# Top-k attention with a GELU layer on one Trainium2 core: last query rows squared on DVE and turned over through DRAM

## The chip, the core and the metric

The kernel runs on one core of a Trainium2 chip. The core has five engines that run side by side, each through its own list of instructions in order: TensorE (PE, matmuls and transposes; its weight loads are shown as PEld), VectorE (DVE), ScalarE (ACT), GpSimd (POOL) and SyncE (SP). Here SP does little but issue DMA transfers, one after another; an issue that has to wait for another engine holds back every later issue in SP's list. The metric is the device time of one execution in microseconds (us), lower being better. Times of the kernel before: 1479.85, 1480.17 and 1480.43 us.

## What is computed

Two blocks in a row, all in float32. The first is attention that keeps, for each query row, only the 32 largest of its 576 scores; the second is a two-layer network with an exact GELU.

```python
B, H, S, D = 8, 8, 576, 64
scores = (1 / sqrt(D)) * q @ k.T                     # per batch and head, 576 x 576
kth    = 32nd largest of each row
scores = where(scores >= kth, scores, -1e9)
attn   = exp(scores - row max) / (row sum + 1e-9)
x      = (attn @ v), heads side by side              # (8 * 576) x 512
out    = gelu(x @ w_in) @ w_out                      # 512 -> 2048 -> 512
```

## The kernel before

**Items.** A batch has 8 heads, taken as 4 pairs. The 576 query rows of a head are cut into four blocks of 128 (`t` = 0 to 3, `NM` = 4) and a last block of 64 (`TL`). An item of the list `items` is one tile of scores with 128 partitions and 2 x 576 columns (`s`, 1152 columns): for `t < NM` one block of 128 rows of the two heads of a pair, side by side. The 64 last rows of a head fill only half the partitions, so a last item (`t == NM`) takes two pairs, `r` = 0 and 1, each with two heads, `e` = 0 and 1: four quarters of 64 partitions by 576 columns. Head `e` of pair `r` stands in the partitions `half(r, e)`, the lower half where `r == e`. In the kernel before, the columns are divided by pairs: columns 0 to 575 hold pair 0, columns 576 to 1151 pair 1.

There are 144 items, 18 for a batch. Two batches make a ring of 36 items; the first batch of a ring has its two last items at the end, the second at its beginning, so four last items stand one behind the other: items 16 to 19 of each ring of 36, which over the kernel are 16 to 19, 52 to 55, 88 to 91 and 124 to 127.

**Slots.** The program is written out by hand in slots: the loop `for n in range(ahead)` emits, for each engine, the work of slot `n`. In slot `n`, DVE finds the 32 largest scores of item `n` (`top_k`: rounds of MAX8 and MATCH_REPLACE8, with the row's smaller and larger halves sorted apart first by `larger` on DVE and `sum_up` and `smaller` on POOL). ACT makes item `n-1` into exponentials (`select`, `softmax`) and POOL completes its row sums (`add_small`). At the end of `top_k(n)` DVE takes the reciprocal of those sums (`inverse(n-1)`, L504), which waits for POOL's L510 and through it for ACT; behind it POOL scales item `n-1` (`normalise`, L552). So DVE and POOL start each slot together, at the reciprocal. PE makes the scores of items `n+2` and `n+3` in even slots (`scores`, L386 and L401, copied from PSUM to `s` by ACT in L394 and L406), and turns over item `n-2` (`transposes`), since the product with v needs the probabilities with keys on partitions. What is left of PE's time goes to the pieces of the network (`mlp`: `h_ps` in L773, `seven` and `y_ps` in L927 and L929), a given number for each slot.

**Turning over.** There are two ways. By PE: eight 128 x 128 transposes (L649), a transpose of the tail columns (L619, or two of 64 columns in L622 for a last item), and copies by ACT to the tile `pt` (L664, L629; the tails of a last item go in two copies, L635, to a tile of their own, `pt_end`). Or, where `squared(i)` holds, by DVE and DRAM: `square_p` transposes 32 x 32 squares within `s` on DVE (L569, in the middle of `top_k` of slot `i+2`), `write_p` sends the tile to DRAM in four DMAs (L579, at the end of slot `i+2`), and `read_p` brings it back with its squares in order in four more (L586, at the beginning of slot `i+3`). Before the change `squared(i)` holds for every other item with `t < NM` from item 28 on, 48 in all. `pt` has one buffer; it holds two items with `t < NM` (one squared, one turned over by PE), whose product `attend` (L715) follows in the slot after.

**The product of a last item.** `attend(n-3)` in slot `n` multiplies `pt` and `pt_end` with v, two heads of two pairs (L726), and ACT copies the result to `xT` (L731, `copy_x`). For the first batch of a ring it then loads v of the same pairs of the next batch into the same tiles (`issue(load("v", ...))`), eight DMAs on SP (L131, L134) for an item. `issue` runs a load at once, unless `held[0]` is set: in a slot whose item `n-2` is squared, loads wait in `late_issues` until `flush()`, behind `write_p(n-2)`.

**PSUM.** The transposes, the products, `seven` and the tail scores share one bank in turn (`bank`, tag "z"); the first scores of a slot use tag "pr", the second scores (`second=True`) and `h_ps` share tag "l1".

Of the kernel before, what the change touches and what calls it, by code (L numbers as in the profile page):

```python
# [14 lines left out]
def kernel(  # L15
# [19 lines left out]
    nc = tc.nc  # L35
    f32, i32, u32 = mybir.dt.float32, mybir.dt.int32, mybir.dt.uint32
    bf16, i16, u16 = mybir.dt.bfloat16, mybir.dt.int16, mybir.dt.uint16
    AF = mybir.ActivationFunctionType
# [295 lines left out]

        return slice((r ^ e) * TL, ((r ^ e) + 1) * TL)

    def halves(t, e, step):

        return spread(t[:, e * TL :], step + (TL if e == 0 else -TL), TL)

    def pair_tile(name, tag="pr"):
        return ps.tile([P, 2, 512], f32, tag=tag, bufs=1, name=name)

    def last_keys(i, t_ps):

        pair, t = items[i]
        s = S_of[i]
        if t < NM:
            nc.tensor.matmul(
                t_ps[:, 0:P], lhsT=q_of[pair][:, t * P : (t + 1) * P],  # L350
                rhs=kt_of[pair][:, SM : SM + P], start=True, stop=True,
            )
            if i == 0:
                return lambda: nc.vector.tensor_scalar(
                    s[:, SM : S + TL], t_ps[:, 0:P], scale, None, op0=ALU.mult
                )
            return lambda: nc.scalar.activation(
                s[:, SM : S + TL], t_ps[:, 0:P], func=AF.Copy, scale=scale
            )
        for r in range(2):  # L360
            kt = kt_of[pair + r]
            for e in range(2):
                nc.tensor.matmul(
                    t_ps[half(r, e), r * TL : (r + 1) * TL],
                    lhsT=kt[:, SM + P + e * TL : SM + P + (e + 1) * TL],
                    rhs=kt[:, SM + e * TL : SM + (e + 1) * TL],
                    start=True, stop=True,
                )
        return lambda: nc.scalar.activation(
            s.rearrange("p (r n) -> p r n", r=2)[:, :, SM:S],  # L370
            t_ps[:, 0:P].rearrange("p (r n) -> p r n", r=2), func=AF.Copy, scale=scale,
        )

    def scores(i, second=False):
        if i >= N or i in S_of:
            return
        pair, t = items[i]
        S_of[i] = s = work.tile([P, 2 * S], f32, tag="s", bufs=6, name="s")
        s_ps = pair_tile("s_ps", "l1" if second else "pr")
        if not few[0]:  # L380
            last_keys(i, bank("t_ps"))()
        if t < NM:
            q_t, kt = q_of[pair][:, t * P : (t + 1) * P], kt_of[pair]
            for e in range(2):
                rows = slice(e * D, (e + 1) * D)
                nc.tensor.matmul(  # L386
                    s_ps[:, e], lhsT=q_t[rows, :], rhs=kt[rows, 0:SM], start=True, stop=True
                )
# [5 lines left out]
            nc.scalar.activation(spread(s, S + TL, SM), s_ps, func=AF.Copy, scale=scale)  # L394
# [12 lines left out]

    lists_of = {}
    HS = S // 2
# [171 lines left out]
    def read_p(i):  # L581

        if squared(i):
            d = turned.pop(i)
            for k in range(P // SQ):
                nc.sync.dma_start(  # L586
                    out=pt_now[0][k * SQ : (k + 1) * SQ, :, 0:P], in_=d[:, :, k, :]
                )

    def transposes(i):  # L590
# [14 lines left out]
        def tails(ahead):  # L605
# [1 line left out]
            keys = last_keys(ahead, tp) if ahead is not None and ahead < N else None  # L607
            at = P
            if t % 2 == 0:
                pt_now[0] = work.tile([P, 2 * NM + 1, 2 * P], f32, tag="pt", bufs=1, name="pt")  # L610
            if diag is not None:
                for e in range(2):
                    nc.tensor.matmul(
                        tp[e * TL : (e + 1) * TL, at : at + P],
                        lhsT=s[:, SM + e * TL : SM + (e + 1) * TL], rhs=diag[:, e],
                        start=True, stop=True,
                    )
            elif t < NM:
                nc.tensor.transpose(tp[:, at : at + P], s[:, SM : S + TL], ident)  # L619
            else:  # L620
                for r in range(2):
                    nc.tensor.transpose(  # L622
                        tp[0:TL, at + r * P : at + (r + 1) * P],
                        s[:, r * S + SM : (r + 1) * S], ident,
                    )
            if keys:
                keys()
            if t < NM:
                nc.scalar.copy(  # L629
                    out=pt_now[0][:, NM, t % 2 * P : (t % 2 + 1) * P], in_=tp[:, at : at + P]  # L630
                )
                return
            for e in range(2):
                c = slice(e * TL, (e + 1) * TL)
                nc.scalar.copy(  # L635
                    out=halves(pt_end[c, 0, :], e, P),
                    in_=halves(tp[0:TL, at : at + 2 * P], e, P),
                )

        x = t % 2 * P if t < NM else 0  # L640

        def turn_over(tp, e):
            first = e * (S + TL if t < NM else S)
# [52 lines left out]
    def attend(i):  # L696
# [24 lines left out]
        else:  # L721
            for r in range(2):
                vt = raw_of("v", pair + r)
                for j in range(NJ):
                    for e in range(2):
                        nc.tensor.matmul(  # L726
                            o[e * D : (e + 1) * D, r * TL : (r + 1) * TL], lhsT=vt[:, j, e, :],
                            rhs=pt[:, r * NJ + j, half(r, e)] if j < NM else pt_end[:, r, half(r, e)],
                            start=(j == 0), stop=(j == NJ - 1),
                        )  # L730
            copies.append(lambda: nc.scalar.copy(  # L731
# [588 lines left out]
```

## Time and profile before

| | |
|---|---|
| median of 3 runs | 1480.17 us |
| profiled execution, its own time | 1479.73 us |
| its span | 1478.0 us |
| busy time of PE, DVE, ACT, POOL | 1461.6, 1294.3, 1099.9, 1140.1 us |
| DMA packets, bytes | 477645, 112.94 MB |
| share of 16 DMA engines that SP's queue took | 35.3% |

The span runs from the first to the last instruction; the 1.7 us between it and the time of that execution lie around it. In the profile, "L649" is a line of the kernel before; a row names the engine, the operation, the tile written and the tiles read, and the shape. Rows of the timeline begin with the start in us from the start of the span and the time that the instructions took together; a bracket at the end tells how long the engine had been idle and which engine's instruction ended that. A float32 matmul shows as two records (x2), a transpose as one. A row of windows gives the length of a stretch and then the busy time of each engine in it.

### The profile page before, as it was taken

What the parts mean: (1) busy time and instruction counts of PE and PEld (TensorE: products, weight loads), DVE (VectorE), ACT (ScalarE), POOL (GpSimd) and SP (SyncE); (2) the same over time, 40 slices, a digit from 0 to 9 for tenths busy, and PEclk for the clock granted to TensorE, in tenths of its full rate; (3) what the DMA queues carried; (4) which work ended last, traced back from release to release, by engine and by line L of the source; (5) the groups of instructions that cost most, each with busy time, mean ns of one, the idle gap of its engine ahead of it and who ended that gap; (6) DMA issues with size and microseconds to landing.
All of it is one profiled execution on the core that took longest, in us unless ns stands there. A gap on an engine that the chain in (4) does not pass through costs nothing. (4 is left out here: it accounts for less than half of the span.)

```text
span 1478.0 us, 27006 instructions
## 1 busy us (share of the span) xinstructions
PE 1461.6 (99%) x8817; PEld 1147.9 (78%) x8817; DVE 1294.3 (88%) x3318; ACT 1099.9 (74%) x1942; POOL 1140.1 (77%) x1291
## 2 busy tenths in 40 slices
PE   8999999999999999999999999999999999999999
PEld 6876677877777777887777778787777777787787
DVE  8999899999999988999999987999999997998701
ACT  7999977877777687777777778777777777776620
POOL 6877567877898879877898978886788887987732
PEclk9999999999999999999999999999999999999999
DMA  7424310045435322345534331345453421233300
GB/s 198 143 86 124 84 48 1 24 88 101 95 73 93 66 58 52 65 95 108 105 83 81 69 61 47 66 93 99 97 103 73 89 55 41 61 61 72 70 15 15
DMA packets 477645, 112.94 MB, mean 76 GB/s; under 512 B 413216, under 2 KB 469056, under 8 KB 477504
## 3 DMA queue, kind: packets, MB, share of 16 engines
q1 hardware_dynamic: 476240, 110.78, 35.3%
q8 instruction: 70, 1.15, 0.3%
q14 instruction: 71, 0.58, 0.1%
q10 hardware_dynamic: 1200, 0.39, 0.1%
q0 software_dynamic: 64, 0.03, 0.0%
HBM read 73.39 MB, written 37.75 MB: 75 GB/s over the span
## 5 line engine op out<-in xcount | busy, mean ns | idle before, releaser
L773 PE MATMUL h_ps<-xT,w_in_sb 128*128 128x256 f32 (+1 forms) x2560 | 536.2, 361 | 0.1
L773 PEld LDWEIGHTS h_ps<-xT,w_in_sb 128*128 128x128 f32 x2560 | 436.5, 190 | 73.4 <-issue 25.2
L483 DVE MAX8 top<-lists 128x8 f32<-128x576 f32 (+1 forms) x792 | 476.4, 641 | 0.0
L486 DVE MATCH_REPLACE8 lists<-top,lists 128x288 f32<-128x288 f32 (+1 forms) x528 | 307.9, 589 | 0.0
L552 POOL TENSOR_TENSOR s<-s,rden 128x1152 f32<-128x1152 f32 x135 | 285.8, 2117 | 0.3 <-DVE rden L504 0.3
L529 ACT ACTIVATE s<-s,bias 128x576 f32<-128x576 f32 x288 | 225.4, 787 | 11.0 <-issue 0.4
L517 ACT ACTIVATE s<-s,neg 128x576 f32<-128x576 f32 x288 | 225.5, 793 | 1.7 <-POOL neg L497 1.6
L510 POOL TENSOR_SCALAR den<-den 128x2 f32<-128x2 f32 x144 | 31.4, 218 | 215.9 <-ACT s L529 210.2
L455 POOL TENSOR_TENSOR lists<-lists 128x576 int32<-128x576 int32 x132 | 186.2, 1410 | 4.0
L447 POOL TENSOR_TENSOR lists<-s 128x576 int32<-128x576 int32 x133 | 187.2, 1407 | 0.0
L715 PE MATMUL o<-pt,raw_v 128*64 128x256 f32 x1280 | 153.0, 384 | 1.8 <-ACT s L529 1.1
L715 PEld LDWEIGHTS o<-pt,raw_v 128*64 128x64 f32 x1280 | 87.8, 136 | 85.8 <-issue 37.2
L789 ACT ACTIVATE g<-h_ps 128x512 f32<-128x512 f32 x144 | 78.2, 594 | 100.6 <-PE h_ps L773 100.4
L929 PE MATMUL y_ps<-w_out_sb,sum 128*128 128x256 f32 x472 | 140.4, 379 | 0.0
L394 ACT ACTIVATE s<-s_ps 128x1024 f32<-128x1024 f32 x127 | 125.5, 1035 | 10.5 <-PE s_ps L386 10.3
L664 ACT COPY pt<-tp 128x1024 f32<-128x1024 f32 x85 | 86.6, 1019 | 62.2 <-PE tp L649 62.1
L386 PE MATMUL s_ps<-kt,qm 64*128 64x512 f32 x512 | 129.4, 618 | 0.8 <-ACT s L392 0.8
L504 DVE RECIPROCAL rden<-den 128x2 f32<-128x2 f32 x144 | 23.2, 161 | 108.6 <-POOL den L510 107.4
L486 DVE MATCH_REPLACE8 lists<-first,lists 128x288 f32<-128x288 f32 x264 | 114.3, 439 | 0.0
L929 PE MATMUL y_ps<-w_out_sb,g 128*128 128x256 f32 x480 | 113.4, 379 | 0.0
L483 DVE MAX8 first<-lists 128x8 f32<-128x288 f32 x268 | 106.6, 436 | 0.0
L929 PEld LDWEIGHTS y_ps<-w_out_sb,g 128*128 128x128 f32 x480 | 91.2, 190 | 12.4
(167 smaller groups left out, 2533.1 us busy)
## 6 DMA issues: line engine op xcount, KB each, us to landing
turned<-s SPq DMA_DIRECT2D x192, 144.0 KB, 3.5
pt<-turned SPq DMA_DIRECT2D x192, 144.0 KB, 3.2
raw_v<-in_v_dram SPq DMA_DIRECT2D x64, 128.0 KB, 2.4
out_dram<-y SPq DMA_DIRECT2D x30, 256.0 KB, 2.1
raw_q<-in_q_dram SPq DMA_DIRECT2D x112, 64.0 KB, 2.0
raw_k<-in_k_dram SPq DMA_DIRECT2D x112, 64.0 KB, 2.0
w_out_sb<-in_moe_w_in_dram SPq DMA_DIRECT2D x14, 511.8 KB, 4.8
w_out_sb<-in_moe_w_out_dram SPq DMA_DIRECT2D x10, 511.8 KB, 4.1
```

Source lines behind the costliest of these rows:

```text
L386: nc.tensor.matmul(s_ps[:, e], lhsT=q_t[rows, :], rhs=kt[rows, 0:SM], start=True, stop=True)
L394: nc.scalar.activation(spread(s, S + TL, SM), s_ps, func=AF.Copy, scale=scale)
L447: nc.gpsimd.tensor_tensor(t[:, :, 1].bitcast(i32), a.bitcast(i32), b.bitcast(i32), op=ALU.add)
L455: nc.gpsimd.tensor_tensor(into_of(i)[:, :, 1].bitcast(i32), both, top, op=ALU.subtract)
L483: nc.vector.max(x[:, e], src[:, e])
L486: nc.vector.match_replace(dst[:, e], x[:, e], src[:, e], LOWEST)
L517: nc.scalar.activation(s, s, func=AF.Prelu, bias=st["neg"][:, e : e + 1], scale=1.0, alpha=STEEP)
L529: nc.scalar.activation(s, s, func=AF.Exp, bias=st["bias"][:, e : e + 1], scale=1.0, accum_out=st["den"][:, e : e + 1],)
L552: nc.gpsimd.tensor_tensor(s, s, wide, op=ALU.mult)
L715: nc.tensor.matmul(o[e * D : (e + 1) * D, 0:n], lhsT=vt[:, j, e, :], rhs=pt[:, e * NJ + j if j < NM else NM, :], start=(j == 0), stop=(j = ...
L773: nc.tensor.matmul(h_tile(u)[:, i, :], lhsT=w_in_sb[:, ko, f * P : (f + 1) * P], rhs=xT[:, ko, c0 : c0 + n], start=(ko == 0), stop=(ko == ...
L929: nc.tensor.matmul(acc[names][:, k], lhsT=lhsT, rhs=rhs, start=(j == 0 and k == 0), stop=(j == FT // 2 - 1 and k == 1),)
```

## The change

`squared(i)` now also holds for the last items between item 27 and item 141, that is for twelve of the sixteen (items 52 to 55, 88 to 91 and 124 to 127), besides the 48 from before. For these items `delayed(i)` holds too: `attend(n-4)`, ahead of `read_p` and of the scores in slot `n`, takes the place of `attend(n-3)`, behind the scores. `read_p` now takes the tile `pt` itself, where before the slot of `transposes` did.

For the squares to come out in the order that `read_p` expects, the columns of a last item now hold heads instead of pairs: columns 0 to 511 are head 0, 512 to 639 the tails of both heads, 640 to 1151 head 1, as in the other items. `scores`, `last_keys`, `attend` and `transposes` follow that. The tail of a last item is then one block of 128 columns, turned over by one PE transpose and one copy into `pt` where PE does it (items 16 to 19), and `pt_end` with its memset goes.

```diff
     def last_keys(i, t_ps):
...
-                    t_ps[half(r, e), r * TL : (r + 1) * TL],
+                    t_ps[half(r, e), e * TL : (e + 1) * TL],
...
-            s.rearrange("p (r n) -> p r n", r=2)[:, :, SM:S],
-            t_ps[:, 0:P].rearrange("p (r n) -> p r n", r=2), func=AF.Copy, scale=scale,
+            s[:, SM : S + TL], t_ps[:, 0:P], func=AF.Copy, scale=scale
...
     def scores(i, second=False):
...
-                        s_ps[half(r, e), r, :], lhsT=kt[rows, SM + P + e * TL : SM + P + (e + 1) * TL],
+                        s_ps[half(r, e), e, :], lhsT=kt[rows, SM + P + e * TL : SM + P + (e + 1) * TL],
...
-            s2 = s.rearrange("p (r n) -> p r n", r=2)
-            nc.scalar.activation(s2[:, :, 0:SM], s_ps, func=AF.Copy, scale=scale)
+            nc.scalar.activation(spread(s, S + TL, SM), s_ps, func=AF.Copy, scale=scale)
...
-    pt_end = const.tile([P, 2, P], f32, name="pt_end")
-    nc.gpsimd.memset(pt_end, 0.0)
 
     def squared(i):
 
-        return SINGLE.stop - 2 < i < N - 2 and i % 2 == 0 and items[i][1] < NM and i % RINGS != 12
+        if not SINGLE.stop - 2 < i < N - 2:
+            return False
+        return items[i][1] == NM or (i % 2 == 0 and i % RINGS != 12)
+
+    def delayed(i):
+
+        return squared(i) and items[i][1] == NM
+
+    def pt_tile():
+        return work.tile([P, 2 * NM + 1, 2 * P], f32, tag="pt", bufs=1, name="pt")
...
         if squared(i):
             d = turned.pop(i)
+            pt_now[0] = pt_tile()
...
             def keys_only(ahead):
-                pt_now[0] = work.tile([P, 2 * NM + 1, 2 * P], f32, tag="pt", bufs=1, name="pt")
...
-            elif t < NM:
+            else:
                 nc.tensor.transpose(tp[:, at : at + P], s[:, SM : S + TL], ident)
-            else:
-                for r in range(2):
-                    nc.tensor.transpose(
-                        tp[0:TL, at + r * P : at + (r + 1) * P],
-                        s[:, r * S + SM : (r + 1) * S], ident,
-                    )
...
-            for e in range(2):
-                c = slice(e * TL, (e + 1) * TL)
-                nc.scalar.copy(
-                    out=halves(pt_end[c, 0, :], e, P),
-                    in_=halves(tp[0:TL, at : at + 2 * P], e, P),
-                )
+            nc.scalar.copy(out=pt_now[0][:, NM, x : x + P], in_=tp[:, at : at + P])
...
-                            rhs=pt[:, r * NJ + j, half(r, e)] if j < NM else pt_end[:, r, half(r, e)],
+                            rhs=pt[:, e * NJ + j if j < NM else NM, half(r, e)],
...
         held[0] = n < N and squared(n - 2)
+        product = delayed(n - 4) and attend(n - 4)
         read_p(n - 3)
...
-        product = attend(n - 3)
+        if not delayed(n - 3):
+            product = attend(n - 3) or product
```

In the lists of instructions that the two programs give to the engines, this is what comes of it for items 52 to 55 (the other two groups alike). PE loses ten transposes an item; the pieces of the network stay in the slots in which they were; the product of each item stands a slot later, and in the even slots it stands ahead of the two items' scores, with L773 directly behind them. SP's list, which held sixteen v loads and two stores of `y` here, becomes (W for the four DMAs of `write_p`, R for the four of `read_p`, V for eight loads of v, by item): W52, R52, W53, R53, W54, V, R54, W55, V, two stores of `y`, R55, W56. POOL's list stays as it was but for the memset.

More of the change, by code (lines that the diff above doesn't have):

```diff
@@ L335, in half @@
         return slice((r ^ e) * TL, ((r ^ e) + 1) * TL)
-    def halves(t, e, step):
-        return spread(t[:, e * TL :], step + (TL if e == 0 else -TL), TL)
     def pair_tile(name, tag="pr"):
@@ L609, in tails @@
             if t % 2 == 0:
-                pt_now[0] = work.tile([P, 2 * NM + 1, 2 * P], f32, tag="pt", bufs=1, name="pt")
+                pt_now[0] = pt_tile()
             if diag is not None:
@@ L617, in tails @@
                     )
-            elif t < NM:
+            else:
                 nc.tensor.transpose(tp[:, at : at + P], s[:, SM : S + TL], ident)
-            else:
-                for r in range(2):
-                    nc.tensor.transpose(
-                        tp[0:TL, at + r * P : at + (r + 1) * P],
-                        s[:, r * S + SM : (r + 1) * S], ident,
-                    )
             if keys:
                 keys()
-            if t < NM:
-                nc.scalar.copy(
-                    out=pt_now[0][:, NM, t % 2 * P : (t % 2 + 1) * P], in_=tp[:, at : at + P]
-                )
-                return
-            for e in range(2):
-                c = slice(e * TL, (e + 1) * TL)
-                nc.scalar.copy(
-                    out=halves(pt_end[c, 0, :], e, P),
-                    in_=halves(tp[0:TL, at : at + 2 * P], e, P),
-                )
-        x = t % 2 * P if t < NM else 0
+            nc.scalar.copy(out=pt_now[0][:, NM, x : x + P], in_=tp[:, at : at + P])
+        x = t % 2 * P
         def turn_over(tp, e):
-            first = e * (S + TL if t < NM else S)
+            first = e * (S + TL)
             for j in range(NM):
```

## The prediction, made before the changed kernel ran

> **What bounds the kernel now.** I read the page first, for the busy times; then windows of busy time over the five slots around items 52 to 55; then the timeline of each engine there.
>
> ```profile
> PE 1461.6 (99%) x8817; PEld 1147.9 (78%) x8817; DVE 1294.3 (88%) x3318; ACT 1099.9 (74%) x1942; POOL 1140.1 (77%) x1291
> ```
>
> PE is busy 99% of the span. A busy PE is not always a full one, so the slots decide.
>
> ```profile
> core 0: us, PE busy (x) PEld busy (x) DVE busy (x) ACT busy (x) POOL busy (x), PEclk, DMA share, GB/s
> 526.87:536.93 10.06, 10.06 (x64) 8.27 (x58) 8.09 (x23) 6.46 (x13) 9.35 (x12) 1.00 0.05 8
> 536.93:549.24 12.31, 12.31 (x107) 9.61 (x107) 8.09 (x23) 10.44 (x23) 5.91 (x7) 1.00 0.22 50
> 549.24:559.51 10.27, 10.25 (x116) 8.97 (x113) 8.10 (x23) 7.05 (x15) 10.03 (x13) 1.00 0.27 60
> 559.51:569.65 10.14, 10.14 (x58) 7.78 (x58) 8.09 (x23) 9.53 (x18) 9.98 (x13) 1.00 0.14 53
> 569.65:578.89 9.24, 9.24 (x79) 8.24 (x76) 9.24 (x24) 6.59 (x13) 8.53 (x10) 1.00 0.29 44
> ```
>
> These are slots 54 to 58, cut at DVE's reciprocals. In slots 54 to 57 items 52 to 55 go over PE: PE never waits, DVE works only 8.09 us of each. Slot 58 has a square and DVE fills it: 9.24 us. POOL fills slots 56 and 57 (10.03 of 10.27, 9.98 of 10.14), which no saving elsewhere can shorten. The rows that show the join of the engines:
>
> ```profile
> 536.76 0.17 DVE L504 RECIPROCAL rden<-den 128x2 f32<-128x2 f32 x1 [1.97 <-POOL den L510]
> 549.07 0.17 DVE L504 RECIPROCAL rden<-den 128x2 f32<-128x2 f32 x1 [4.22 <-POOL den L510]
> 573.39 1.36 DVE L569 STREAM_TRANSPOSE s<-s 128x1152 f32<-128x1152 f32 x1
> 536.51 0.22 POOL L510 TENSOR_SCALAR den<-den 128x2 f32<-128x2 f32 x1 [0.55 <-ACT s L529]
> ```
>
> DVE waits 1.97 us in slot 54 and 4.22 in slot 55 for sums that come late over ACT from PE; in slot 54 POOL itself waits only 0.55. So there is room for a square on DVE in these slots, and PE is the bound.
>
> **What PE is spared.** An item's transposes, from start to the next start:
>
> ```profile
> 543.14 0.38 PE L622 MATMUL tp_t<-ident,s 128*64 128x128 f32 x2
> 543.36 0.60 PE L929 MATMUL y_ps<-w_sum,sum 128*128 128x256 f32 x2
> ...
> 544.22 1.04 PE L649 MATMUL tp<-ident,s 128*128 128x128 f32 x8
> 545.10 0.60 PE L929 MATMUL y_ps<-w_sum,g 128*128 128x256 f32 x2
> ```
>
> 0.22 + 0.88 = 1.10 us an item, 4.4 us for each group of four, 13.2 us in all. Items 16 to 19 lose one transpose of 0.11 us each, 0.4 us; DVE waits little there, so I take 0.3 (between 0 and 0.4). POOL's memset goes at the start, under loads: nothing. ACT's copies go with the transposes; they only shorten ACT.
>
> **What DVE pays.** Slot 58 against 8.09 us of work: 9.24 - 8.09 = 1.15 us a square. Slot 54 then ends when POOL lets it, 0.5 us sooner (at 536.4); slot 55 takes 9.25 instead of 12.31 and ends at 545.65, 3.6 us sooner; slots 56 and 57 stay at POOL's 10.27 and 10.14, which hide the squares, and end at 555.9 and 566.1.
>
> **Where the product comes.** It is no longer made from what ACT copied, but from what eight DMAs bring. PE's rows for the product, the scores and what follows, and ACT's copies of the scores:
>
> ```profile
> 546.92 1.99 PE L386 MATMUL s_ps<-kt,qm 64*128 64x512 f32 x8
> ...
> 557.80 0.69 PE L726 MATMUL o<-pt,raw_v 128*64 128x64 f32 x16
> ...
> 559.12 1.13 PE L773 MATMUL h_ps<-xT,w_in_sb 128*128 128x256 f32 x4
> 560.08 1.03 PE L927 MATMUL seven<-w_sum,g 128*128 128x256 f32 x4
> ...
> 567.54 1.99 PE L386 MATMUL s_ps<-kt,qm 64*128 64x512 f32 x8
> 569.45 0.69 PE L726 MATMUL o<-pt,raw_v 128*64 128x64 f32 x16
> ...
> 570.77 2.86 PE L773 MATMUL h_ps<-xT,w_in_sb 128*128 128x256 f32 x12
> ...
> 573.68 4.48 PE L773 MATMUL h_ps<-xT,w_in_sb 128*128 128x256 f32 x20
> 578.00 1.03 PE L927 MATMUL seven<-w_sum,g 128*128 128x256 f32 x4
> ```
>
> ```profile
> 568.71 1.94 ACT L394 ACTIVATE s<-s_ps 128x1024 f32<-128x1024 f32 x2 [0.21 <-PE s_ps L386]
> ```
>
> A product takes 1.32 us (569.45 to 570.77; likewise 557.80 to 559.12). Today it also covers something: the second scores share the PSUM tag "l1" with `h_ps`, so L773 must wait for the second L394, which ends at 570.65, while the product runs until 570.77. With the product ahead of the scores that cover is gone: 3.23 us from the first scores to L773 (567.54 to 570.77), of which the scores themselves are 1.91 (to 569.45). So PE newly waits 1.3 us in slots 56 and 58.
>
> SP's rows for the transfers (the first two from a place where four v loads, for one pair, stand behind a write; then the eight of an item, here and in the next ring):
>
> ```profile
> 325.04 0.90 SPq L131 DMA_DIRECT2D raw_v<-in_v_dram  x1
> ...
> 327.58 0.51 SPq L134 DMA_DIRECT2D raw_v<-in_v_dram  x1
> ...
> 537.89 0.39 SPq L131 DMA_DIRECT2D raw_v<-in_v_dram  x1
> ...
> 542.97 0.47 SPq L134 DMA_DIRECT2D raw_v<-in_v_dram  x1
> ...
> 567.12 1.05 SPq L844 DMA_DIRECT2D out_dram<-y  x2
> 574.82 3.40 SPq L579 DMA_DIRECT2D turned<-s  x4
> 580.89 2.55 SPq L586 DMA_DIRECT2D pt<-turned  x4
> ...
> 885.97 0.39 SPq L131 DMA_DIRECT2D raw_v<-in_v_dram  x1
> ...
> 890.13 0.47 SPq L134 DMA_DIRECT2D raw_v<-in_v_dram  x1
> ```
>
> ```profile
> 1390.89 2.54 SPq L586 DMA_DIRECT2D pt<-turned  x4
> ```
>
> ```profile
> 1396.21 2.16 PE L715 MATMUL o<-pt,raw_v 128*64 128x256 f32 x18 [1.08 <-ACT s L529]
> ```
>
> A write starts 574.82 - 569.65 = 5.17 us after its slot; a read can start 580.89 - 574.82 = 6.07 after the write, when that has landed; a product can start 5.32 us after the read's first issue (1390.89 to 1396.21: PE waits there, and ACT, which the bracket names, had nothing to do with `pt` of a squared item). SP needs 3.40 us to issue a write, 2.55 for a read, 1.05 for the stores. Eight v loads take 5.55 (537.89 to 543.44) or 4.63 (885.97 to 890.60), and four behind a write 3.05 (325.04 to 328.09), so that eight behind a write (V) lie between 4.6 and twice 3.05, 6.1. I take 5.35, the middle. With gaps of 0.05 between groups:
>
> - Item 52: write at 526.87 + 5.17 = 532.0, read at 538.1, product from 543.4. PE, with 2.2 us saved and one product less ahead, is there at 546.92 - 2.2 - 1.32 = 543.4. No wait.
> - Item 53: write at 536.4 + 5.17 = 541.6, read 547.65, product from 553.0. PE: from 543.4 on the 10.88 us that now lie between 546.92 and 557.80, less 1.1, plus 1.3 to 2.0 for ACT's copies (the second waits until write 53 has landed and freed its `s`): 555.1. No wait.
> - Item 54: write at 545.65 + 5.17 = 550.8, issued until 554.25. Now V stands ahead of the read, since the load is held until behind the write: 554.3 to 559.65. Read at 559.7, though the data had landed at 556.9; product from 565.0. PE: 555.1 + 9.74 - 1.1 = 563.75. **Wait 1.25 us.**
> - Item 55: SP is free at 562.3, write until 565.75, V until 571.15, stores until 572.25, read 572.3, product from 577.6. PE: 565.0 + 1.32 + 3.23 + 2.91 + 0.8 of 4.32 = 575.95. **Wait 1.65 us.**
>
> The product ends at 578.95, the last L773 takes 0.96 (559.12 to 560.08), and L927 starts at 579.9, where it starts at 578.00 now: 1.9 us later. Of that, a wait that PE has today a little further on goes away:
>
> ```profile
> 581.46 0.38 PE L349 MATMUL tp_t<-kt,qm 128*128 128x128 f32 x2
> 581.97 0.33 PE L619 MATMUL tp_t<-ident,s 128*128 128x128 f32 x1
> ```
>
> 581.97 - 581.46 - 0.22 = 0.3 us. **Net 1.6 us later for each group of four.** From there PE sets the pace as before, and DVE, 3.4 us ahead, waits for it. The chain that decides is SP's: from write 54 to product 55 it is issue after issue with no gap, while the 4.4 us saved on PE become waits for `pt` and for ACT's copies.
>
> The sum: 3 x 1.6 - 0.3 = +4.5 us against the profiled execution's own 1479.73 us, so 1484.2; the median of the runs lies 0.44 above that execution, so **1484.6 us** (+0.3%). The bounds of V (4.6 to 6.1, two of them a group) move it by -4.5 and +4.5: 1480 to 1489.
>
> **A rule weighed.** The first matmuls of the kernel stand in the trace at another rate than the later ones of the same shape:
>
> ```profile
> L1113 PE MATMUL warm<-ident x276: 275/275/377, 15.2 to 92.3; 128*128 128x128 f32 x138
> L1113 PE MATMUL warm<-raw_v x18: 421/421/580, 1.0 to 4.8; 128*128 128x128 f32 x18
> ```
>
> They are slow until some 5 us, and no later wait here (1.08 us at 1396.21) brought the slow rate back. The Trainium skill, page "TensorE: Matmul & The Clock Gate", section "Part 1: The HAM clock gate (the "warmup" mystery)", says that an idle window of about 3.4 us puts PE back to half rate. By it the waits of 1.3 to 2.0 us forecast here would not trip the gate and the sum stays 1484.6; two waits running into one would, which is rival (d) below.
>
> **Rivals.** (a) *The reads are in time.* If SP gets through V in 3.9 us or less each (5.35 less half of the 1.25 + 1.65), or PE comes later than I think, only the waits for ACT's copies remain: 4.4 - 2 x 1.3 = 1.8 us gained a group, and the 0.3 at L619: 3 x 2.1 + 0.3 = 6.6 us, 1473.6. For it: items 52 and 53 are in time in my own sum. Against it: V stands in SP's list between W54 and R54, and 3.9 us is below the shortest of today's rows. (b) *The gain is had in full*, to what DVE and POOL allow: 3.4 us a group, 1480.2 - 10.5 = 1469.7. It needs (a) and L773 not held by ACT's copies; the tag speaks against it. (c) *It cancels*: a chain 1.5 us shorter than mine, 1480. (d) *Slower, by PE's clock*: if a wait reaches the point where PE slows (the waits for 54 and ACT's copies in slot 58 joining past 3 us), each group has matmuls at 421 instead of 275 ns for some 4 us, as at the start, 1.4 us or more for each of two waits: 3 x 2.8 more, 1493. The granted clock is 1.00 in all rows today, and the forecast waits are half as long. (e) *Late reads run on into slot 60*: write 56 can only start behind read 55, at 574.9, its product at 586.3, where PE comes some 3 us later; it takes 3 us more of delay than forecast to begin, so little chance, and 3 x 3 us more: 1493.6. That the change doesn't do what it says (twelve squares) has next to no chance: SP's list shows the DMAs.
>
> **How the numbers follow.** Forecast 0.61, (a) 0.14, (b) 0.04, (c) 0.10, (d) 0.06, (e) 0.05. The forecast's own range is 1480 to 1489; most of (a) lies below, so the range goes from 1476 to 1490. About 0.2%, 3 us, is what can be told from no change. Faster by more: (a) nearly all and (b), 0.17. Within 3 us of 1480.2: (c), and the lower third of the forecast's range, whose upper limit is 1483.1: 0.27. Slower: the rest, 0.56.
>
> **What would show it.** Sixty squares of 1.36 us; DVE's waits at the reciprocal in slots 54 to 57 gone but for POOL's. PE waits of 1 to 2 us ahead of L726's products of items 54 and 55 of each group, none ahead of 52 and 53; L773 idle 1.3 us behind the scores of slots 56 and 58, released by ACT. On SP, reads 54 and 55 issued the moment the v loads and stores end, though their writes landed earlier; then a wait of DVE of some 5 us in slot 59. If the reads start at their writes' landing instead, or PE's idle time in slots 54 to 59 adds up to less than 4.4 us a group, the forecast is wrong and (a) is right. If PEclk drops, (d).

## The result, and the profile after

The changed kernel takes 1490.20 us (median of 4 runs, 1489.46 to 1490.83) against 1480.30 us (1479.85 to 1480.84) for the kernel before, run beside it: a ratio of 1.0067, with a 95% interval of 1.0049 to 1.0084. It is slower by about 9.9 us, where 4.4 were forecast. Its profiled execution took 1489.96 us, 10.2 more than the one before, and that is the difference taken apart here.

Windows over the slots 54 to 59 of the kernel after, cut at DVE's reciprocals as before (length, then busy time of PE, PE's weight loads, DVE, ACT and POOL, then the clock granted to TensorE):

```profile
core 0: us, PE busy (x) PEld busy (x) DVE busy (x) ACT busy (x) POOL busy (x), PEclk, DMA share, GB/s
526.57:536.16 9.59, 9.59 (x56) 7.78 (x53) 9.36 (x23) 6.54 (x11) 9.35 (x12) 1.00 0.37 56
536.16:545.42 9.26, 9.26 (x79) 7.64 (x79) 9.22 (x23) 7.49 (x17) 5.91 (x7) 1.00 0.60 123
545.42:555.92 10.50, 9.45 (x77) 7.14 (x74) 9.44 (x24) 5.65 (x11) 10.12 (x12) 1.00 0.61 118
555.92:566.05 10.13, 7.08 (x34) 5.92 (x32) 9.35 (x23) 7.20 (x13) 9.97 (x13) 1.00 0.64 143
566.05:577.13 11.08, 10.12 (x73) 7.70 (x74) 9.35 (x23) 5.44 (x10) 8.65 (x11) 0.85 0.76 170
577.13:590.91 13.78, 12.17 (x95) 9.90 (x96) 8.10 (x22) 8.60 (x16) 5.90 (x7) 1.00 0.55 113
```

Up to slot 57 this is the forecast: slot 55 lasts 9.26 us instead of 12.31, DVE is filled with squares, and slots 56 and 57 stay at POOL's pace. But PE, which was idle for 0.02 us in slots 54 to 58 before, is idle for 1.05, 3.05, 0.96 and 1.61 us in slots 56 to 59 (length less busy time), 6.7 us in all. Slot 59 takes 13.78 us, and only 8.10 of them are work for DVE. In slot 58 the granted clock is 0.85 on average.

Which transfers PE waits for stands in its own timeline, with SP's beside it. First PE: the products of items 53, 54 and 55 with the work behind them, then those of items 54 and 55 of the next two groups.

```profile
554.29 1.39 PE L711 MATMUL o<-pt,raw_v 128*64 128x64 f32 x40 [0.44 <-DMA pt<-turned]
...
566.74 2.14 PE L711 MATMUL o<-pt,raw_v 128*64 128x64 f32 x40 [3.73 <-DMA pt<-turned]
568.80 2.81 PE L381 MATMUL s_ps<-kt,qm 64*128 64x512 f32 x8
571.88 2.86 PE L758 MATMUL h_ps<-xT,w_in_sb 128*128 128x256 f32 x12 [0.27 <-ACT s L389]
...
580.03 1.39 PE L711 MATMUL o<-pt,raw_v 128*64 128x64 f32 x40 [1.61 <-DMA pt<-turned]
...
582.31 1.03 PE L912 MATMUL seven<-w_sum,g 128*128 128x256 f32 x4
...
918.33 2.16 PE L711 MATMUL o<-pt,raw_v 128*64 128x64 f32 x40 [3.06 <-DMA pt<-turned]
...
931.32 1.39 PE L711 MATMUL o<-pt,raw_v 128*64 128x64 f32 x40 [1.30 <-DMA pt<-turned]
...
1269.32 1.68 PE L711 MATMUL o<-pt,raw_v 128*64 128x64 f32 x40 [3.95 <-DMA pt<-turned]
...
1282.52 1.39 PE L711 MATMUL o<-pt,raw_v 128*64 128x64 f32 x40 [1.81 <-DMA pt<-turned]
```

SP's list in the first group, from write 53 to read 55 (L580 are writes, L588 reads, L131 and L134 v loads, L829 stores of `y`):

```profile
541.56 4.39 SPq L580 DMA_DIRECT2D turned<-s  x4
548.83 2.85 SPq L588 DMA_DIRECT2D pt<-turned  x4
551.78 3.47 SPq L580 DMA_DIRECT2D turned<-s  x4
555.29 0.89 SPq L131 DMA_DIRECT2D raw_v<-in_v_dram  x1
...
560.84 0.51 SPq L134 DMA_DIRECT2D raw_v<-in_v_dram  x1
561.46 2.57 SPq L588 DMA_DIRECT2D pt<-turned  x4
564.14 3.44 SPq L580 DMA_DIRECT2D turned<-s  x4
...
573.18 1.00 SPq L829 DMA_DIRECT2D out_dram<-y  x2
574.28 2.60 SPq L588 DMA_DIRECT2D pt<-turned  x4
```

From 551.78 to 574.28 us SP issues without a gap, so each read goes out when the list gets to it. The product of item 55 is the last to come, at 580.03, and L912 follows at 582.31, where the kernel before had it at 578.00. From there the lateness goes through ACT, which works in order: the copy of the product, then the gelu, then item 58's exponentials, whose sums POOL and DVE wait for. ACT, then POOL:

```profile
581.46 0.27 ACT L716 COPY xT<-o 128x128 f32<-128x128 f32 x1 [4.62 <-PE o L711]
```

```profile
590.71 0.22 POOL L504 TENSOR_SCALAR den<-den 128x2 f32<-128x2 f32 x1 [7.72 <-ACT s L523]
```

DVE's reciprocals at the end of the first and of the third group, before and after:

```profile
587.00 0.17 DVE L504 RECIPROCAL rden<-den 128x2 f32<-128x2 f32 x1
...
1283.17 0.17 DVE L504 RECIPROCAL rden<-den 128x2 f32<-128x2 f32 x1
```

```profile
590.96 0.17 DVE L498 RECIPROCAL rden<-den 128x2 f32<-128x2 f32 x1 [5.68 <-POOL den L504]
...
1293.44 0.17 DVE L498 RECIPROCAL rden<-den 128x2 f32<-128x2 f32 x1 [5.88 <-POOL den L504]
```

4.0 us late after the first group, 7.2 after the second (942.24 for 935.08), 10.3 after the third: the whole difference arises in the three groups, and between them nothing is made good.

### The profile page after: what moved, and what is told of

It reads as the page before. It is cut to its first block, busy times and chain, and to the rows that moved or that the text cites. A ratio compares the mean times of both kernels' runs of the same rounds, so it can differ in the third digit from the quotient of the medians.

```text
span 1488.1 us, 26925 instructions
## 1 busy us (share of the span) xinstructions
PE 1452.2 (98%) x8693; PEld 1136.5 (76%) x8693; DVE 1309.5 (88%) x3330; ACT 1080.9 (73%) x1902; POOL 1139.9 (77%) x1290
## 4 chain that ended last, share of the span: by engine, by line
PE 52%; POOL 7%; DVE 6%; SPq 3%; DMA 2%; ACT 2%; issue 2%; DVEq 0%; ACTq 0%; POOLq 0%
PE h_ps L758 19%; PE y_ps L914 12%; PE o L700 6%; PE s_ps L381 4%; PE tp L634 3%; DVE top L477 2%; PE seven L912 2%; POOL s L546 2%; DVE lists L480 2%; DMA pt<-turned 2%; PE y_ps L876 1%; PE y_ps L879 1%; POOL lists L441 1%; SPq L588 1%; SPq L580 1%
## 5 line engine op out<-in xcount | busy, mean ns | idle before, releaser
L758 PE MATMUL h_ps<-xT,w_in_sb 128*128 128x256 f32 (+1 forms) x2560 | 535.2, 361 | 1.4 <-ACT s L389 1.3
L758 PEld LDWEIGHTS h_ps<-xT,w_in_sb 128*128 128x128 f32 x2560 | 437.0, 190 | 79.5 <-issue 25.2
L649 ACT COPY pt<-tp 128x1024 f32<-128x1024 f32 x73 | 74.3, 1017 | 54.1 <-PE tp L634 54.0
L416 DVE TENSOR_TENSOR lists<-s 128x576 f32<-128x576 f32 x133 | 100.7, 758 | 0.0
```

Of the source, the lines that this page charges most:

```text
L758: nc.tensor.matmul(h_tile(u)[:, i, :], lhsT=w_in_sb[:, ko, f * P : (f + 1) * P], rhs=xT[:, ko, c0 : c0 + n], start=(ko == 0), stop=(ko == ...
```

## The experiments

Ratios are against the kernel before, run on the same chip, with the 95% interval. "The kernel after" is the changed kernel, and each diff is against it unless another is named. Three theories were set against their rivals: SP's order makes the reads late (1); the half clock that shows behind the longest waits costs its own share (2); the place of the product ahead of the scores costs PE waits for ACT's copies (3).

### Half of the v loads issued by ScalarE

```diff
-                issue(lambda r=r: load("v", pair + r + NP))
+                by = nc.scalar if delayed(i) and (r == 0 or i % RINGS % 4 == 1) else None
+                issue(lambda r=r, by=by: load("v", pair + r + NP, by))
```

> The v loads behind the products of items 16 and 17 leave SP's list: four of the first eight and all of the second eight are issued by ScalarE instead, at the same place of the program; nothing else is changed. Theory 1 (the reads of items 18 and 19 are late because they stand behind sixteen v loads in SP's order): the four reads of item 18 are issued about 3 us earlier, when the write has landed, and those of item 19 about 4 us earlier; the product of item 18 waits under 1.2 us instead of 3.1 to 4.0, that of item 19 under 0.5 instead of 1.3 to 1.8, no stretch at half clock is left, and the time is 1470 to 1479 us. Rival 1 (the reads are late because the v loads' bytes share the DMA engines with them): the bytes move in the same stretch, so the reads take that much longer from issue to landing, the waits stay above 2.5 us and the time stays within 1487 to 1492. Rival 2 (ScalarE pays for the issuing): the copies of xT and the gelu of the next slot come late, TensorE waits for them instead, and the time is 1480 to 1488.

Measured: 1506.87 us, 1.0181 (1.0167 to 1.0195), worse than any of the cases. The four v loads that stayed on SP, and what they waited for by the view of waits in 545 to 600 us:

```profile
556.97 0.39 SPq L131 DMA_DIRECT2D raw_v<-in_v_dram  x1
560.57 0.52 SPq L134 DMA_DIRECT2D raw_v<-in_v_dram  x1
565.37 0.40 SPq L131 DMA_DIRECT2D raw_v<-in_v_dram  x1
566.78 0.50 SPq L134 DMA_DIRECT2D raw_v<-in_v_dram  x1
```

```profile
SPq L131 <- DMA raw_v<-in_v_dram: 4.3, 1, 4.3
SPq L134 <- DMA turned<-s: 3.2, 1, 3.2
```

They are issued in 0.4 to 0.5 us each, but one has waited 4.3 us for another v load and one 3.2 us for a write. In the program's lists of instructions the transfers of SP and ScalarE share eight semaphores, handed out in turn, and a transfer waits until the one that had its semaphore before has landed. Split over two engines, SP's loads wait for loads that ScalarE issues a slot later. So this edit added waits and tells theory 1 from neither rival; it shows that SP's list is made of landings as well as of issue times. The Trainium skill, page "DMA: Bandwidth & Descriptors", section "Issuing engines are not separate DMA queues", says that issuing from several engines only saves sequencer time; here it cost 16.7 us against the kernel after, through the semaphores.

### Keeping PE busy through the wait

```diff
+        if delayed(n - 4) and (n - 4) % RINGS == 18:
+            z = bank("warm")
+            for _ in range(12):
+                nc.tensor.matmul(z[:, 0:P], lhsT=ident, rhs=ident, start=True, stop=True)
         product = delayed(n - 4) and attend(n - 4)
```

> Twelve matmuls of 128 columns that compute nothing stand ahead of the product of item 18 in each group, so that TensorE works through some 2.6 us of the wait of 3.1 to 4.0 us. Both theories expect a granted clock of 1.00 in the slot behind it, and that product and the four score matmuls behind it at their usual 1.4 and 2.0 us instead of 2.1 and 2.8. Theory 2 (the half clock costs its 1.6 us in every group): the seventh product of the next slot starts 1.6 us earlier and the time falls to about 1485.5 (1484 to 1487). Rival (what sets the next slot is SP's list, which does not hang on TensorE's pace there: the product of item 19 waits for its reads until the same moment): its wait grows by about 1.6 us, and the time stays at 1488.5 to 1491.

Measured: 1491.99 us (1491.16 to 1494.84), 1.0082 (1.0069 to 1.0096). PE at the products of items 54 and 55, and of item 127 (the last of the third group); then windows behind the product of item 55:

```profile
566.47 1.39 PE L711 MATMUL o<-pt,raw_v 128*64 128x64 f32 x40 [0.53 <-DMA pt<-turned]
...
579.89 2.40 PE L711 MATMUL o<-pt,raw_v 128*64 128x64 f32 x40 [3.31 <-DMA pt<-turned]
...
1287.45 1.39 PE L711 MATMUL o<-pt,raw_v 128*64 128x64 f32 x40 [2.50 <-DMA pt<-turned]
```

```profile
579.40:582.80 3.40, 2.91 (x41) 2.74 (x42) 3.40 (x8) 0.45 (x2) 2.06 (x2) 0.50 0.91 135
582.80:586.20 3.40, 3.40 (x9) 2.70 (x8) 0.85 (x2) 2.35 (x4) 0.00 (x0) 0.50 0.13 35
```

The rival holds. The product of item 54 runs at its usual 1.39 us and saves what the half clock cost, and the next product starts at 579.89 instead of 580.03: PE waits 3.31 us there instead of 1.61. In the third group no half clock is left at all (2.50 us of waiting, clock 1.00 behind it), and by DVE's reciprocals that group still costs 3.8 us, against 3.1 in the kernel after. Behind item 54 the half clock was free, because SP's list set the next product anyway. Behind item 55's product nothing covers it: here 6.8 us at 0.50. The profiled execution is the slowest of its four, so the windows show more than the median's price.

### Scores first

```diff
-        product = delayed(n - 4) and attend(n - 4)
-        read_p(n - 3)
+        product = False
+        if not delayed(n - 4):
+            read_p(n - 3)
...
+        if delayed(n - 4):
+            product = attend(n - 4)
+            read_p(n - 3)
         if not delayed(n - 3):
             product = attend(n - 3) or product
```

> The product of a last item, and the reads that follow it in the program, stand behind the slot's score matmuls again instead of ahead of them. Theory 3 (the order costs 1.3 us in each of two slots of a group, for ScalarE's copies of the scores, and the score matmuls would cover most of the wait for reads): the wait of h_ps for ScalarE falls from 1.3 us to the 0.3 of other slots, the product of item 18 waits under 1.5 us, no half clock is left, and the time falls to 1480 to 1485. Rival (SP's list sets when the reads of item 19 land, whatever TensorE does before): TensorE is early in vain, the product of item 19 waits 4 us or more instead of 1.3 to 1.8, a half-clock stretch may appear behind that wait, and the time stays within 1487 to 1491.

Measured: 1492.58 us, 1.0086 (1.0072 to 1.0099): the rival again. The product of item 55 starts at 579.12, only 0.9 us sooner, after a wait that the trace puts at 4.81 us:

```profile
579.12 2.40 PE L711 MATMUL o<-pt,raw_v 128*64 128x64 f32 x40 [4.81 <-DMA pt<-turned]
```

Its 2.40 us show the half clock in the place where it costs. With the first edit added:

> Both edits together: the v loads shared out between SP and ScalarE, and the product behind the score matmuls. If theory 1 and theory 3 both hold, no product waits more than 0.5 us, no half clock is left, ScalarE's copies are covered, and the full saving of about 1.1 us of TensorE for each of twelve items comes through: 1467 to 1472 us. If only theory 1 holds, the time is that of the first kernel of this group, within 1 us. If VectorE's slots set the pace once TensorE is faster, it is 1472 to 1477 with VectorE never idle in the group.

Measured: 1498.64 us, 1.0125 (1.0111 to 1.0139), none of the three cases: it carries the same crossed semaphores as the first kernel.

### The v loads left out

```diff
-                issue(lambda r=r: load("v", pair + r + NP))
+                if not delayed(i):
+                    issue(lambda r=r: load("v", pair + r + NP))
```

> The sixteen v loads behind the products of items 16 and 17 are left out of every group, so the output of the pairs that would use them is computed from stale v; nothing else is changed, and all products, writes and reads run as before. Theory 1 (SP's order and the eight DMA semaphores that its transfers take in turn make the reads late): the reads of item 18 are issued at the landing of its write, near 558.6 us instead of 561.5, the product of item 18 waits 0.3 to 1.2 us instead of 3.1 to 4.0; the reads of item 19 go out near 571.5 instead of 574.3, and its product starts near 576.5 to 577.5 instead of 580.0. As the time moves with that last product, it falls by about 3 times 2.5 to 3.5 us, to 1480 to 1483. What is then left over the forecast saving is the time from the square to the product (write, landing, reads, landing), which no order on SP shortens. Rival (the reads are late for the bytes of other transfers, or something off SP sets the last product): 1487 to 1491.

Measured: 1472.78 us (1472.72 to 1473.56), 0.9949 (0.9936 to 0.9961), faster still than theory 1 asked. SP's reads and PE's products of items 54 and 55:

```profile
557.89 2.54 SPq L588 DMA_DIRECT2D pt<-turned  x4
...
568.04 2.55 SPq L588 DMA_DIRECT2D pt<-turned  x4
```

```profile
563.18 1.39 PE L711 MATMUL o<-pt,raw_v 128*64 128x64 f32 x40 [0.27 <-ACT s L523]
...
573.65 1.39 PE L711 MATMUL o<-pt,raw_v 128*64 128x64 f32 x40 [0.38 <-issue]
```

The reads go out 3.6 and 6.2 us sooner and the products come 3.6 and 6.4 us sooner. So the sixteen loads and what they bring with them in SP's list, in three groups, are worth 17.4 us against the kernel after: more than the whole loss. This run removes their bytes too, but the reads themselves are hardly faster without them: from read to product 5.29 us pass for item 54 and 5.61 for item 55, against 5.28 and 5.75 in the kernel after. So contention for the DMA engines can explain only a small part of their lateness. The next kernel keeps all the bytes.

### The loads moved within SP's list

```diff
+                f = lambda r=r: load("v", pair + r + NP)
+                if not delayed(i) or r == 1:
+                    issue(f)
+                elif i % 2 == 0:
+                    f()
+                else:
+                    behind_read.append(f)
...
         read_p(n - 3)
+        while behind_read:
+            behind_read.pop()()
```

> All on SP again: the first four of each eight v loads are issued earlier. Those behind item 16's product go ahead of item 17's reads, where SP stands idle until a write lands; those behind item 17's product go right behind item 18's reads instead of behind item 19's write. Theory 1: the reads of item 18 go out near 558.6 instead of 561.5 us and its product waits 0.4 to 1.3 us at a clock of 1.00; the reads of item 19 go out near 572 and its product starts near 577.5 instead of 580.0, after a wait of 2.5 to 3.5 us, since TensorE is there earlier; the time is 1480 to 1486. Rival (the transfers' bytes are what makes the reads late): moved loads cost the neighbours as much, the waits of both products stay as they are within 0.5 us, 1488 to 1491.

Measured: 1485.74 us, 1.0038 (1.0025 to 1.0051), within theory 1's range. All bytes move as before; the product of item 54 starts at 564.84 after 1.40 us, and that of item 55 at 578.16. Order alone gives back 4.5 us. With the product behind the scores as well:

> The last kernel's order on SP, and the product with its following reads behind the slot's score matmuls. Theory 1 (the end of a group is set by item 19's square, write and reads): item 18's product waits nothing, ScalarE's copies cost 0.3 us instead of 1.3, and all of that is waited for again at item 19's product, 4 us or more, with a half-clock stretch behind it that falls on the path: 1482 to 1488, no faster than the last kernel. Theory 3 (the place of the product sets the group's end): 2.5 us less per group than the last kernel, 1474 to 1478.

Measured: 1484.08 us, 1.0024 (1.0015 to 1.0033): theory 1's range, and 1.7 us faster than the last kernel, where theory 1 asked for nothing and theory 3 for 7.5.

### Two items instead of four

```diff
-        return items[i][1] == NM or (i % 2 == 0 and i % RINGS != 12)
+        if items[i][1] == NM:
+            return i % RINGS >= 18
+        return i % 2 == 0 and i % RINGS != 12
```

> Only items 18 and 19 of each group go by squares and DRAM; items 16 and 17 go by TensorE's transposes again, their products in the slot they had before. The v loads behind item 16's product then stand ahead of the writes, those behind item 17's still between item 18's write and reads. Theory 1: TensorE pays back 2.2 us a group, but is that much later at item 18's product, which then waits 1 to 2.5 us instead of 3.1 to 4.0 without a half clock; item 19's product starts near 577 us: 1480 to 1486. Rival (each late item costs its own share, whatever stands beside it): half of the excess of 9.9 us over the kernel before, and half of the saving, so 1484 to 1488 with the waits of both products as they are.

Measured: 1492.77 us, 1.0083 (1.0068 to 1.0099): neither. Half of the change costs more than the whole. PE's product of item 54 and SP's read for it:

```profile
568.00 2.27 PE L713 MATMUL o<-pt,raw_v 128*64 128x64 f32 x40 [4.52 <-DMA pt<-turned]
```

```profile
562.68 2.57 SPq L590 DMA_DIRECT2D pt<-turned  x4
```

With slot 55 back at 12 us (item 53 goes over PE), write 54 starts only at 553.84; eight v loads still follow it, and the read goes out at 562.68, 1.2 us later than in the kernel after. My expectation had moved PE and left SP where it was. Item 55, with no v loads ahead, is in time (its product at 579.60 shows no wait), so the loss is one read behind one set of v loads, and the half clock that its wait brings: 3.4 us at half rate, which no later wait covers here.

### Fewer loads, and stores held

On top of the kernel with half of the loads moved and the scores first, the two stores of `y` between write and read 55 are held for a slot:

```diff
-        run_stores()
+        if not delayed(n - 2) or not (n - 2) % 4 == 3:
+            run_stores()
```

> The kernel with half of the v loads moved and the product behind the score matmuls, with one more edit: the two stores of y that stand between item 19's write and its reads are held until behind the reads. Theory 1: the reads of item 19 go out 1.0 us earlier, and as the group's end hangs on them alone, the time falls by 3 times 1.0 us, from 1484 to about 1481 (1480 to 1482.5). Rival (a place in SP's list costs nothing there, since the reads wait for the write's landing anyway): 1483.5 to 1485.

Measured: 1481.62 us, 1.0009 (1.0000 to 1.0018), as theory 1 had it: two stores, 1.0 us of SP's list, are worth 2.5 us in three groups. In the next kernel the stores are held and the scores come first too, but all six loads of item 17 stand behind write 55, and the loads are fewer, since the last 64 rows of both pairs come in one transfer for each head (`both_v` holds two pairs in one tile):

```diff
...
+            if tails:
+                nc.sync.dma_start(
+                    out=t[e * TL : (e + 1) * TL, :, NM, e, :],
+                    in_=v[b, h0 + e : h0 + 4 : 2, SM:S].rearrange("r p d -> p r d"),
+                )
...
+            if delayed(i) and pair + NP < n_pairs:
+                mains = lambda: load_v(pair + NP, False)
+                mains() if i % 2 == 0 else issue(mains)
+                issue(lambda: load_v(pair + NP, True))
```

> Three edits on SP's list, and the product behind the score matmuls. The eight v loads behind item 16's product and behind item 17's become six each (the last 64 rows of two pairs come in one transfer); the first four behind item 16 go ahead of item 17's reads, the six behind item 17 stand behind item 19's write; the slot's two stores of y are held until the next slot, behind item 19's reads. Theory 1 (the length of SP's list between item 19's square and its reads sets the group's end): the reads of item 19 go out near 568.5 us (574.3 in the kernel after, 570.9 in the kernel that moved half of the loads and the product, 568.0 without v loads), its product starts near 574, no clock under 1.00, and the time is 1472 to 1477, faster than the kernel before by 0.3 to 0.6%. Rival (the reads of item 19 cannot start sooner, or the product then waits for its v): the product stays at 576 or later and the time within 1480 to 1485.

Measured: 1476.86 us (1475.83 to 1481.19), 0.9983 (0.9974 to 0.9992): theory 1 by its median. The same with the product ahead of the scores:

> The last kernel with the product and its following reads ahead of the score matmuls, where the change put them. Theory 3 (that place costs 1.3 us of waiting for ScalarE's copies in two slots of a group): 1.3 to 2.6 us slower per group than the last kernel wherever nothing else sets the group's end, 1476 to 1483 in all. Rival (item 19's reads set the group's end in both): the same time as the last kernel within 1.5 us.

Measured: 1476.35 us (1475.81 to 1477.11), 0.9973 (0.9963 to 0.9983): no slower, where theory 3 asked for 1.3 to 2.6 us more in each group, so theory 3 falls at that size. This is the fastest kernel that computes everything, 0.27% under the kernel before. Its reads on SP and its products on PE for items 54 and 55:

```profile
558.36 2.66 SPq L606 DMA_DIRECT2D pt<-turned  x4
...
569.78 2.55 SPq L606 DMA_DIRECT2D pt<-turned  x4
```

```profile
563.70 1.39 PE L729 MATMUL o<-pt,raw_v 128*64 128x64 f32 x40
...
575.14 1.39 PE L729 MATMUL o<-pt,raw_v 128*64 128x64 f32 x40 [1.33 <-DMA pt<-turned]
```

Read 55 goes out 4.5 us sooner than in the kernel after, its product starts 4.9 us sooner, and the granted clock is 1.00 in all three groups. Last, without v loads and with the scores first and the stores held:

> The kernel without the sixteen v loads of a group (so the output of the pairs that use them comes from stale v), with the product behind the score matmuls and the two stores held until behind item 19's reads. If TensorE's saving of 1.1 us for each item comes through in full once no transfer is late, 1468 to 1471 us; if the pace of the slots is VectorE's and GpSimd's (10.5 and 10.1 us in two slots, 9.25 in the others) once TensorE is freed, no faster than the kernel without v loads alone, 1472 to 1474.

Measured: 1472.56 us (1471.73 to 1473.14), 0.9947 (0.9933 to 0.9961), within 0.3 us of the kernel without v loads alone. That does not show that the place of the product and the stores no longer matter. By DVE's reciprocals the profiled execution gains 3.0, 2.9 and 0.5 us in the three groups, the one without v loads alone 2.2, 2.6 and 2.3. In the third group here PE's clock is 0.51 from 1260.00 to 1263.40, behind this wait:

```profile
1260.22 0.80 PE L345 MATMUL t_ps<-kt,qm 128*128 128x128 f32 x2 [2.33 <-ACT xT L716]
```

So the two kernels are equal with a stretch of half clock in one of them; what the order alone is worth stays open.

## Why the prediction was wrong in size

The forecast was slower by 1.6 us a group through SP's chain; the direction and the chain were right, and the group costs more than twice that. By its steps:

- **What PE is spared, what DVE pays: right.** PE has 124 instructions fewer (8693 against 8817): ten for each of twelve items and four for items 16 to 19. Slots 54 to 57 end within 0.3 us of the forecast, the last at 566.05 for 566.1.
- **PE newly waits 1.3 us for ACT's copies in slots 56 and 58: wrong.** The prediction, and the words on PSUM ahead of it, let the second scores of a slot share the tag "l1" with `h_ps`; `scores(n + 2, two)` gives it to the first. So L758 waits for the first copy alone, and its bracket at 571.88 reads 0.27 us. The bracket is the evidence; that 1476.35 us with the product ahead of the scores is no slower than 1476.86 behind them fits it. The error made PE come too late in the forecast (563.75 at item 54, where it was free near 563.0), so it hid part of the wait. PE's wait at item 55, 1.61 us for a forecast of 1.65, agrees by chance: the product and PE (578.4 for 575.95) both came 2.4 to 2.5 us later than forecast.
- **SP's chain: right as a mechanism, too short, and this is the term that failed.** Against the forecast, write 54 starts 1.0 us late (551.78 for 550.8), read 54 1.8 (561.46 for 559.7), read 55 2.0 (574.28 for 572.3) and product 55 2.4 (580.03 for 577.6). The 2.4 are: 1.0 since read 53 starts 7.27 us after write 53 and not 6.07, and SP is through with it only at 551.7; 0.8 mostly since V behind write 54 takes 6.1 us, the upper bound, and not 5.35; 0.2 for the rest of the list up to read 55; 0.4 from read to product (5.75 for 5.32). L912 is then 4.3 us later than before and not 1.9, the 2.4 over again, and the end of the first group 4.0 us. The second and third group cost 3.2 and 3.1 us. There read 53 follows its write after 6.26 and 5.99 us, about as forecast, but V is 6.3 and 6.2, and read 55 comes 13.1 and 13.2 us after read 54, where the forecast had 12.6 and the first group 12.8. The three groups come to 10.3 where 4.5 were summed.
- **Rival (d), PE's clock: it came, and cost nothing there.** The waits that were to stay at 1.25 us are 3.73, 3.06 and 3.95, each followed by work at half rate (2.14 us for 1.39, 2.81 for 1.99). "Two waits running into one" was not needed; one late read was enough. But the kernel kept busy through that wait gains nothing, so the loss of the kernel after is the chain's and not the clock's.
- **Rival (a), the reads in time, 1473.6: its price came out, in part by luck.** Without v loads the time is 1472.8. But the price charges 1.3 us twice a group for ACT's copies, which cost 0.27 in that run too; what takes up the difference there was not traced. With the loads the design reaches 1476.35 once they are fewer and stand elsewhere in the list and the stores are held: 13.9 us, against 17.4 for leaving the loads out. What parts the two was not taken apart: it may be issue time that is left over, or the loads' bytes.

So the terms that failed are sizes in SP's chain. V was put at 5.35 us, the middle of bounds of which the upper came from four loads behind a write; it measured 6.1 to 6.3 behind write 54 and 5.5 to 5.9 behind write 55, above the middle each time. The step from a write to its read had one row, 6.07 us, and no bounds; it was 7.27 in the first group. The range moved only V, and these together took the result just past it.

## What to carry to other kernels

When work moves from an engine to transfers, write down the whole list of the queue that issues them, stores and unrelated loads included, and give every landing time bounds of its own: here 22 us of unbroken issuing decided the time, while the engine that was relieved only waited. A transfer that nobody needs soon belongs where the queue waits for a landing, not between a write and the read that returns it; two stores in the wrong place were worth 2.5 us. Shortening a wait off the deciding chain (a warm clock, an earlier product) moves it to the next place, where it may cost more.

## What the runs showed of the hardware

The half clock comes behind waits of PE, but the length of the wait does not settle whether it comes. In the kernel with the stores held, a wait of 2.18 us was followed by it and one of 3.20 us was not; the windows give the granted clock behind each:

```profile
570.58 0.49 PE L345 MATMUL t_ps<-kt,qm 128*128 128x128 f32 x2 [2.18 <-ACT xT L716]
...
1268.46 0.49 PE L345 MATMUL t_ps<-kt,qm 128*128 128x128 f32 x2 [3.20 <-ACT xT L716]
```

```profile
571.00:574.00 3.00, 3.00 (x9) 2.38 (x8) 3.00 (x8) 2.60 (x7) 3.00 (x4) 0.50 0.70 191
1268.50:1271.80 3.30, 3.30 (x16) 2.96 (x17) 3.30 (x8) 3.15 (x7) 3.10 (x4) 1.00 0.83 200
```

The shortest wait with half clock behind it in these runs is 1.87 us (ahead of 918.63 in the kernel with the scores first); the wait of 2.50 us at 1287.45 in the kernel kept busy left the clock at 1.00, and every wait above 3.20 us brought the half clock. A window of the kernel after, from the wait for item 54 through the scores behind the product:

```profile
566.50:571.50 5.00, 4.76 (x48) 3.02 (x48) 5.00 (x15) 0.69 (x1) 4.92 (x5) 0.66 0.84 145
```

By its mean clock, 3.4 us of it are at half rate (5.00 x 0.34 x 2), though PE is busy through nearly all of it. The Trainium skill, page "TensorE: Matmul & The Clock Gate", section "Part 1: The HAM clock gate (the "warmup" mystery)", gives an idle window of about 3.4 us, free-running, before the rate halves; here waits of 1.87 and 2.18 us were enough, so as a limit for a plan its figure is too high. And 6.8 us at half rate behind one wait of 3.31 us, in the kernel kept busy, shows that one wait can cost two such stretches.
